# Filter rows of six group halves placed by DMA between SBUF rows instead of by one-hot products, with the evacuations shared out anew

## The chip, the cores and the metric

One NeuronCore of a Trainium2 chip runs the whole program. The metric is the time of one execution on the device, in microseconds (us), as the median of several runs. A trace of one further execution of each kernel gives its profile; its "span" is a little shorter than the timed execution. All runs are used unless they lie over 1.5% above the fastest of their kernel.

Engine names as in the profile: PE is the matrix engine (PEld its weight loads), DVE the vector engine, ACT the scalar engine, POOL is GpSimd, SP the sync engine, which here only issues DMA transfers (SPq is its queue).

## The reference

```python
# x: (8, 3072, 256); filt_r, filt_i: (1537, 256); w1, w2: (256, 1024); w_out: (1024, 256)
X = np.fft.rfft(x, axis=1)
Y = X * (filt_r + 1j * filt_i)[None, :, :]
y = np.fft.irfft(Y, n=3072, axis=1).reshape(24576, 256)
out = np.maximum(y @ w1, y @ w2) @ w_out
```

## The kernel before

Both Fourier transforms are products with tables, in two stages. The start-up does the forward transform of the first two batch items in eight rounds, one for each group of filter rows; then a long body interleaves the dense layers of one item with the transforms of the next. The change touches the start-up alone.

The filter rows lie in SBUF as `Fs` (96 partitions of 16 rows each), but the multiplication wants them in `F`, where partition 64c + 12q + j holds row 8j + 4b + c of `Fs`, and a partition 32 further on holds the mirrored row in reversed order. In the kernel before PE does this move: for each group `g` and part (real or imaginary) eight products with a one-hot matrix `Sel`, then an evacuation from PSUM to `F`, by ACT in one instruction or by DVE in two.

```python
    def expand_f(g, ri, E, sp=0):
        if E is V:
            pf = [p2.tile([128, 2, D], FP32, tag="px", name="pf", bufs=4) for _ in range(2)]
        else:
            p_ = bank2([128, 2, 2, D], FP32, "pf")
            pf = [p_[:, b] for b in range(2)]
        fs = Fs[ri]
        spin(pf[0].rearrange("p u d -> p (u d)"), sp)
        for b in range(2):
            for c in range(2):
                m = 4 * b + c
                TE.matmul(pf[b][64 * c:64 * c + 32], Sel[:, m], fs[:, 2 * g:2 * g + 2], start=True, stop=True)
                p0 = 64 * c + 32
                if g:
                    TE.matmul(pf[b][p0:p0 + 32], Sel[:, 7 - m], fs[:, 16 - 2 * g:14 - 2 * g:-1], start=True, stop=True)
                else:
                    TE.matmul(pf[b][p0:p0 + 32, 0], Sel[:, 7 - m + c], fs[:, 0], start=True, stop=True)
                    TE.matmul(pf[b][p0:p0 + 32, 1], Sel[:, 7 - m], fs[:, 15], start=True, stop=True)
        f_ = F[:, ri, :, 2 * g:2 * g + 2].rearrange("p b u d -> p b (u d)")
        if E is V:
            for b in range(2):
                V.tensor_copy(f_[:, b], pf[b].rearrange("p u d -> p (u d)"))
        else:
            evac(E, f_, p_.rearrange("p b u d -> p b (u d)"))
```

The eight rounds of the start-up. `first_t1` ends in the evacuation of a transpose ("T1"), `first_s2` makes the products `px` and multiplies them by `F` (`pq`), `first_s3` makes the products `pz`. `prep_wd` is the difference Wd = w1 - w2, which the first dense product `ph` needs.

```python
    load_f0()
    patch_f0()
    first_s1(5, S, 2)
    expand_f(6, 0, V)
    first_t1(1, V)
    first_t1(2, V)
    expand_f(1, 1, S)
    expand_f(7, 0, S)
    table_e(t1)
    pend = []
    for n, g in enumerate(order):
        pend.append(first_s2(g, n in (0, 1, 2, 4, 6)))
        if n < 6:
            first_t1(order[n + 2], V)
        if n == 0:
            tables_pe()
            expand_f(2, 1, S)
        if n < 6:
            expand_f((0, 3, 4, 5, 6, 7)[n], 1, S)
        if n < 2:
            load_x(1, 4 + n)
        if n == 2:
            fix_f()
        if n in (1, 3):
            tables_q(n // 2, S)
        if n in (4, 6):
            prep_wd(n // 2 - 2, *wf)
        if n in (4, 5):
            prep_w(n - 4, V)
        if n > 5:
            prep_w(n - 4, S)
        if n == 5:
            table_g()
        if n > 1:
            first_s3(*pend.pop(0))
    first_s3(*pend.pop(0))
    first_s3(*pend.pop(0), split=True)
# ... the body follows ...
```

## Time and profile before

| | before |
|---|---|
| time, median of 2 runs | 527.7 us (527.67 to 527.74) |
| profiled span | 523.8 us |
| PE busy, mean granted clock | 96% of the span, 0.999 |
| end of the last start-up multiplication on DVE | 43.94 us |
| first dense product `ph` on PE | 48.24 us |

From `ph` on, PE is the bound for the remaining 475 us, and nothing there is edited, so "when does the first `ph` start" measures the start-up with one number. The prediction below shows the lines of the profile from which this is read. In a line of a timeline the columns are: start, duration, engine, source line, operation, output<-inputs, shapes, count, and in brackets the idle time before it and what ended that. The first `ph` of the kernel before:

```profile
48.24 0.62 PE L596 MATMUL ph<-y__1134,Wd 128*128 128x512 bf16 x2 [0.38 <-ACT y__1134 L583]
```

### The profile page before, as it was taken

To read this page: it belongs to the slowest core of one execution; us is meant where nothing else is said; L and a number is where in the kernel's file an instruction comes from. 1 tells how busy PE (TensorE), PEld (TensorE's weight loads), DVE (VectorE), ACT (ScalarE), POOL (GpSimd) and SP (SyncE) were. 2 spreads that over 40 slices of the span, in tenths; PEclk is the share of its full clock that TensorE was granted. 3 is DMA by queue.
4 is the path that set the end of the run, shared out by engine and by line. 5 is a ranking of instruction groups with operands and counts; after the bars stand their busy time and mean duration, and the time that the engine had idled before them with its cause. 6 is when DMAs were issued, how large, how long until landed. Compare 5 with 4: busy or idle time off the path is not lost.

```text
span 523.8 us, 12526 instructions
## 1 busy us (share of the span) xinstructions
PE 504.0 (96%) x5204; PEld 346.5 (66%) x5282; DVE 322.4 (62%) x437; ACT 336.9 (64%) x597; POOL 148.0 (28%) x168
## 2 busy tenths in 40 slices
PE   8988989999999999999999999999999999999997
PEld 3556655666667766676666666676667666677775
DVE  8986567435773476437783588537783588544432
ACT  6786658746885588756675577647675556645542
POOL 6683118264027204530066002720000000000000
PEclk9999999999999999999999999999999999999999
DMA  7990699997798969796798769894467936341212
GB/s 143 280 204 23 176 199 320 334 204 177 232 247 241 208 195 300 229 200 185 219 266 201 182 179 241 266 202 139 143 172 157 176 111 150 100 125 41 82 62 100
DMA packets 74093, 97.03 MB, mean 185 GB/s; under 512 B 5106, under 2 KB 49780, under 8 KB 73044
## 3 DMA queue, kind: packets, MB, share of 16 engines
q1 hardware_dynamic: 63012, 63.72, 52.6%
q0 software_dynamic: 11024, 32.51, 20.1%
q8 instruction: 41, 0.67, 0.6%
q14 instruction: 16, 0.13, 0.1%
HBM read 54.79 MB, written 47.19 MB: 195 GB/s over the span
## 4 chain that ended last, share of the span: by engine, by line
PE 76%; issue 1%; DVE 1%; ACT 0%
PE po L621 30%; PE ph L596 26%; PE po L616 7%; PE pz L447 4%; PE py L580 3%; PE px L469 2%; PE pa L410 2%; DVE pq L474 0%; ACT at L413 0%; DVE ot L623 0%
## 5 line engine op out<-in xcount | busy, mean ns | idle before, releaser
L601 ACT ACTIVATE gt<-ph 128x512 bf16<-128x512 f32 x308 | 182.1, 603 | 125.5 <-PE ph L596 124.0
L621 PE MATMUL po<-Wo,gt 128*128 128x256 bf16 x1536 | 229.8, 273 | 3.4
L621 PEld LDWEIGHTS <-gt 128*128 128x128 bf16 x1536 | 150.2, 98 | 57.6
L474 DVE TENSOR_TENSOR pq<-px,F 120x1024 bf16<-120x1024 f32 x112 | 131.7, 1219 | 32.6 <-PE px L469 32.4
L623 DVE COPY ot<-po 128x512 f32<-128x512 f32 x96 | 66.2, 690 | 103.9 <-PE po L621 102.3
L628 POOL DMA_DIRECT2D out_dram<-ot x47 | 25.8, 548 | 311.0 <-DVE ot L623 298.8
L402 POOL TENSOR_TENSOR xd<-xf 128x512 bf16<-128x512 f32 x72 | 89.1, 1268 | 47.2 <-DMA xf<-in_x_dram 46.2
L596 PEld LDWEIGHTS <-Wd 128*128 128x128 bf16 x768 | 70.8, 98 | 21.2 <-issue 12.6
L451 ACT ACTIVATE zt<-pz 112x512 bf16<-112x512 f32 x112 | 61.0, 602 | 19.5 <-PE pz L447 16.4
L599 DVE TENSOR_SCALAR gt<-ph 128x512 bf16<-128x512 f32 x76 | 52.2, 687 | 29.4 <-PE ph L596 22.0
L413 ACT ACTIVATE at<-pa 128x512 bf16<-128x512 f32 x72 | 39.2, 596 | 15.6 <-PE pa L410 15.4
L580 PE MATMUL py<-G,zr 128*128 128x128 bf16 x384 | 30.1, 219 | 1.9 <-ACT zr L514 0.7
L447 PE MATMUL pz<-pq,VP 56*64 56x256 bf16 x448 | 29.4, 271 | 1.1 <-DVE pq L474 0.8
L580 PEld LDWEIGHTS <-zr 128*128 128x128 bf16 x384 | 25.3, 98 | 5.1 <-issue 3.6
L447 PE MATMUL pz<-pq,VQ 56*64 56x256 bf16 x448 | 28.6, 268 | 0.0
L469 PE MATMUL px<-bt,U 48*64 48x256 bf16 x448 | 23.5, 274 | 1.0 <-DMA bt<-ad 1.0
L469 PEld LDWEIGHTS <-U 48*64 48x64 bf16 x448 | 11.6, 106 | 9.2 <-issue 6.0
L447 PEld LDWEIGHTS <-VP 56*64 56x64 bf16 x448 | 14.1, 105 | 3.7 <-issue 2.4
L530 DVE TENSOR_TENSOR pq<-px,F 120x1024 bf16<-120x1024 f32 x11 | 13.2, 1222 | 3.5 <-ACT F L514 1.9
L410 PE MATMUL pa<-xd,C 64*64 64x512 bf16 x144 | 15.2, 400 | 0.0
L514 ACT ACTIVATE F<-pf 128x1024 bf16<-128x1024 f32 x10 | 10.1, 1032 | 6.7 <-PE pf L134 6.7
L447 PEld LDWEIGHTS <-VQ 56*64 56x64 bf16 x448 | 13.9, 106 | 0.0
(387 smaller groups left out, 591.2 us busy)
## 6 DMA issues: line engine op xcount, KB each, us to landing
out_dram<-ot POOLq DMA_DIRECT2D x47, 512.0 KB, 5.1
xf<-in_x_dram SPq DMA_DIRECT2D x72, 256.0 KB
ad<-at SPq DMA_DIRECT2D x42, 256.0 KB
bt<-ad SPq DMA_DIRECT2D x56, 192.0 KB
zd<-zt SPq DMA_DIRECT2D x56, 192.0 KB
zr<-zd SPq DMA_DIRECT2D x14, 768.0 KB
xb<-in_x_dram POOLq DMA_DIRECT2D x12, 256.0 KB, 10.6
wf<-in_moe_w_dram POOLq DMA_DIRECT2D x2, 1024.0 KB, 10.3
```

The costliest lines, as they stand in the source:

```text
L402: G.tensor_tensor(xb[b, c][:, i], xf[:, 0], xf[:, 1], op)
L413: S.activation(at[:, 2 * m:2 * m + 2], pa[m], AF.Copy)
L447: TE.matmul(pz[c][64 * k:64 * k + 64, i], W[64 * c:64 * c + 56, 2 * g + i, k], pq[k][64 * c:64 * c + 56, ri, i], start=(ri == 0), stop=(ri ...
L451: S.activation(zt[0:ROWS, c, o:o + 2], pz[c][0:ROWS], AF.Copy)
L469: TE.matmul(px[k][64 * c:64 * c + 64, i], U[64 * k:64 * k + 48, 4 * g + 2 * i + c], bt_[64 * k:64 * k + 48, t_], start=True, stop=True)
L474: V.tensor_tensor(pq[k][0:FROWS], px[k][0:FROWS].rearrange("p (o i) d -> p o i d", o=1).to_broadcast([FROWS, 2, 2, D]), F[0:FROWS, :, k, 2 ...
L580: TE.matmul(py[:, n], zr[b][:, 4 * i + n, 128 * dc:128 * dc + 128], G1, start=True, stop=True)
L596: TE.matmul(ph, Wd[:, dc, 128 * j:128 * j + 128], y_[:, dc].rearrange("p a b -> p (a b)"), start=(dc == 0), stop=(dc == 1))
L599: V.tensor_scalar(gt[tt][:, j], ph, 0.0, None, OP.max)
L601: S.activation(gt[tt][:, j], ph, AF.Relu)
L621: TE.matmul(p_, g_[:, jj, 128 * n:128 * n + 128], Wo[:, jj], start=False, stop=(jj == 7))
L623: V.tensor_copy(ot[tt][:, n - 1:n + 1], po[tt])
```

## The change

Its intent is to take work off PE, ACT and DVE in the start-up, where all three are nearly full, by letting the DMA engines place six of the sixteen group halves: imaginary rows of groups 4 to 7, real ones of 6 and 7. The rows that no transfer writes must be zero, hence two clears. The relief is then used to move three T1 evacuations from DVE to ACT and one Wd difference from GpSimd to DVE.

```diff
--- before.py
+++ after.py
@@ -141,6 +141,24 @@
                 V.tensor_copy(f_[:, b], pf[b].rearrange("p u d -> p (u d)"))
         else:
             evac(E, f_, p_.rearrange("p b u d -> p b (u d)"))
+
+    def spread_f(ri, g0):
+        n = 16 - 2 * g0
+        for b in range(2):
+            for c in range(2):
+                m = 4 * b + c
+                for q in range(2):
+                    p0 = 64 * c + 12 * q
+                    nc.sync.dma_start(out=F[p0:p0 + J, ri, b, 2 * g0:16], in_=Fs[ri][m:m + 89:8, 2 * g0:16])
+                    nc.sync.dma_start(out=F[p0 + 32:p0 + 32 + J, ri, b, 2 * g0:16],
+                                      in_=Fs[ri][7 - m:96 - m:8, n:0:-1])
+
+    def clear_f(ri, g0, E):
+        f_ = F[:, ri, :, 2 * g0:16].rearrange("p b u d -> p b (u d)").bitcast(FP32)
+        if E is S:
+            S.activation(f_, zero.rearrange("p (a b) -> p a b", a=1).to_broadcast([128, 2, (16 - 2 * g0) * D // 2]), AF.Copy)
+        else:
+            E.memset(f_, 0.0)
 
     F0 = zpool.tile([64, 2, 2, D], FP32, tag="zt", name="F0")
 
@@ -201,6 +219,7 @@
                         fill=1.0 - 2.0 * q, base=-12 * (1 - q), channel_multiplier=1)
     load_x(0, 4)
     load_x(0, 5)
+    clear_f(0, 6, G)
     load_f(1)
 
     Ct = init.tile([128, 128], BF16)
@@ -337,8 +356,8 @@
         for _ in range(n):
             TE.matmul(pd, Sp, Sp.rearrange("p (o x) -> p o x", o=1).to_broadcast([128, 4, 128]), start=True, stop=True)
 
-    def prep_wd(k, w1f, w2f):
-        G.tensor_tensor(Wd[:, k], w1f[:, k], w2f[:, k], OP.subtract)
+    def prep_wd(k, E, w1f, w2f):
+        E.tensor_tensor(Wd[:, k], w1f[:, k], w2f[:, k], OP.subtract)
 
     def load_wo():
         G.dma_start(out=Wo, in_=moe_w_out.rearrange("(c p) j -> p c j", p=128))
@@ -644,6 +663,7 @@
     zeros(At[:, :, 48:64].rearrange("p h m t -> p h (m t)"), [4, 512])
     zeros(U.rearrange("p t (q x) -> p (t q) x", q=2)[:, :, 24:32], [64, 8])
     zeros(VP.rearrange("p u b n -> p (u b) n")[:, :, 48:64], [32, 16])
+    clear_f(1, 4, S)
     bt[0] = bpool.tile([128, T, D], BF16, tag="bt", name="bt")
     uu, mk, t1 = tables_u()
     done = []
@@ -671,30 +691,32 @@
     load_f0()
     patch_f0()
     first_s1(5, S, 2)
-    expand_f(6, 0, V)
+    expand_f(1, 1, S)
     first_t1(1, V)
     first_t1(2, V)
-    expand_f(1, 1, S)
-    expand_f(7, 0, S)
+    spread_f(1, 4)
+    spread_f(0, 6)
+    expand_f(2, 1, S)
     table_e(t1)
     pend = []
     for n, g in enumerate(order):
         pend.append(first_s2(g, n in (0, 1, 2, 4, 6)))
         if n < 6:
-            first_t1(order[n + 2], V)
+            first_t1(order[n + 2], (V, S)[n > 2])
         if n == 0:
             tables_pe()
-            expand_f(2, 1, S)
-        if n < 6:
-            expand_f((0, 3, 4, 5, 6, 7)[n], 1, S)
+        if n < 2:
+            expand_f((3, 0)[n], 1, S)
         if n < 2:
             load_x(1, 4 + n)
         if n == 2:
             fix_f()
-        if n in (1, 3):
-            tables_q(n // 2, S)
-        if n in (4, 6):
-            prep_wd(n // 2 - 2, *wf)
+        if n in (1, 2):
+            tables_q(n - 1, S)
+        if n == 3:
+            prep_wd(0, V, *wf)
+        if n == 6:
+            prep_wd(1, G, *wf)
         if n in (4, 5):
             prep_w(n - 4, V)
         if n > 5:
```

## The prediction

> **What bounds the kernel now.** I read the engine rows of the page first, then the chain that ended last, then the busy time by stage, then the timelines of the vector engine and of the sync engine's DMA queue in the first 48 us, where the whole change lies.
>
> ```profile
> span 523.8 us, 12526 instructions
> PE 504.0 (96%) x5204; PEld 346.5 (66%) x5282; DVE 322.4 (62%) x437; ACT 336.9 (64%) x597; POOL 148.0 (28%) x168
> PE po L621 30%; PE ph L596 26%; PE po L616 7%; PE pz L447 4%; PE py L580 3%; PE px L469 2%; PE pa L410 2%; DVE pq L474 0%; ACT at L413 0%; DVE ot L623 0%
> ```
>
> From about 114 us to the end the chain is almost nothing but PE (L621, L596, L616: the dense layers). Nothing in that body is edited. The first dense product (ph, L596) starts at 48.24 us in the PE timeline, and the stretches of 50 us after 100 us show PE busy for 48.9 and 49.2 of 50. So the start-up before 48 us can only move the end by moving the moment at which the body starts, and then nearly one for one.
>
> The start-up by stage (columns: stretch, length, busy PE, PEld, DVE, ACT, POOL, granted clock, DMA share, GB/s):
>
> ```profile
> 20.00:30.00 10.00, 8.95 (x163) 5.32 (x157) 7.96 (x15) 8.22 (x11) 7.55 (x8) 1.00 1.12 299
> 30.00:40.00 10.00, 9.00 (x194) 5.51 (x194) 9.10 (x11) 8.16 (x11) 8.42 (x6) 1.00 1.05 186
> 40.00:47.00 7.00, 5.57 (x160) 3.95 (x159) 4.22 (x5) 4.12 (x6) 4.45 (x2) 1.00 0.01 2
> ```
>
> DVE and ACT are both close to full from 20 to 40 us. Just as important: the DMA engines are saturated (1.12, 1.05) until the records of the software queue end at 39.66 us, and idle afterwards. The chain through this stage is eight rounds (groups in the order 1, 2, 3, 4, 5, 0, 6, 7) of products px, multiplication by the filter on DVE (L530), products pz:
>
> ```profile
> 29.92 2.36 DVE L530 TENSOR_TENSOR pq<-px,F 120x1024 bf16<-120x1024 f32 x2 [0.51 <-ACT F L514]
> 33.40 1.22 DVE L530 TENSOR_TENSOR pq<-px,F 120x1024 bf16<-120x1024 f32 x1 [0.53 <-ACT VQ L514]
> 36.20 2.36 DVE L530 TENSOR_TENSOR pq<-px,F 120x1024 bf16<-120x1024 f32 x2 [0.37 <-issue]
> 41.58 2.36 DVE L530 TENSOR_TENSOR pq<-px,F 120x1024 bf16<-120x1024 f32 x2 [0.70 <-issue]
> ```
>
> The first line is group 4: it needs its filter rows at 29.92. The last is group 7; its end, 43.94, releases the last pz and then the body. What feeds it by one-hot products costs, per group and part, an ACT evacuation:
>
> ```profile
> L514 ACT ACTIVATE F<-pf 128x1024 bf16<-128x1024 f32 x10 | 10.1, 1032 | 6.7 <-PE pf L134 6.7
> ```
>
> The queue on which the new transfers will go shows how small transfers fare while the engines are saturated:
>
> ```profile
> 18.59 2.31 SPq L154 DMA_DIRECT2D F<-in_filt_r_dram  x6
> 20.94 5.21 SPq L154 DMA_DIRECT2D F<-in_filt_i_dram  x6
> 27.77 0.24 SPq L157 DMA_DIRECT2D F<-in_filt_i_dram  x1
> 28.06 0.25 SPq L158 DMA_DIRECT2D F<-in_filt_r_dram  x1
> SPq L154 <- DMA F<-in_filt_r_dram: 3.3, 4, 2.2
> ```
>
> An issue takes 0.24 to 0.4 us, yet the second six took 5.21. In the built program each transfer of this queue waits for the one eight places earlier, and the ninth indeed starts only at 23.85: the first, issued at 18.59, took 5.2 us to land. By the trace's records of single DMA packets its first packet ran at 22.16, 3.5 us after the issue. The two patches, issued at 27.77 and 28.06, have their packets at 31.37 and 31.68, 3.6 us after.
>
> **What the Trainium skill says.** "Perfetto Trace Analysis", DMA Instruction, HWDGE: the profiled time ends when the sequencer has pushed the transfer; movement is not in it. The trace agrees (0.43 us shown, 5.2 us to landing). "DMA: Bandwidth & Descriptors", Queues, rings and completion order: a DMA engine goes round the queues that have work, packet by packet. The trace agrees: from 22.2 us each engine took a packet of this queue about every 0.22 us, one software packet of 4096 bytes (185 ns) and one of its own (some 50 ns). Same page, Why a DMA increments its semaphore by 16: the number of engines divides the slowest dimension; 12 rows make 12 engines, one row each. "TensorE: Matmul & The Clock Gate", Part 1: after an idle window of about 3.4 us the PE clock halves until it has been busy that long. No such gap is in this trace (clock 1.00 throughout).
>
> **The change part by part.** Removed: six expansions. On PE two of them ran from 19.86 to 20.74, so 0.44 each, 2.6 us in all. ACT loses five evacuations, at 0.92 from start to start, 4.6 us; DVE loses two copies of some 0.6, 1.2 us. Moved: three T1 evacuations from DVE to ACT (DVE -1.8, ACT +2.8), one Wd difference from POOL (2.35) to DVE (about 1.25, from the 0.96 of the 768-wide difference at L275). Added: a clear on ACT of about 1.9 us (At's zeros are 2048 wide and took 1.89), which fits into ACT's idle 2.17 us before 9.78; and a memset on POOL, which fits in its later idle 1.76 us. On those engines alone it is a net saving of up to 2 or 3 us.
>
> Also added: 32 transfers on the sync queue, and the changed program's order puts them behind load_f0 and the patches. So none is issued before 28.3 us. Group 4 multiplies at 29.92 today; in the changed program its first half waits for the eight imaginary transfers with b = 0, its second half and the GpSimd half of group 5 for the eight with b = 1. My working of these:
> - Issues. 1 to 6 at 28.35 to 30.1 (their predecessors land by 29.8). Number 7 waits for the first patch (31.6), number 8 for the second (32.0).
> - Service. First packets about 3.5 us after the issue, 32.1. A forward transfer is 1 row of 4 KB and a completion per engine, 2 turns; a reversed one is 8 pieces of 512 bytes and a completion, 9 turns. Four pairs are 44 turns; at 0.21 us (software packets of 2048 bytes, 173 ns, plus some 40) that is 9.2 us: the first eight land at about 41.
> - Second eight. Numbers 9 to 15 queue behind; 16 can only be issued when 8 has landed, 41.5, and lands near 43. Even at no service time, 16 cannot land before 32.0 + 3.7 + 3.7, about 39.5.
> - The sixteen real ones, then on idle engines at some 0.3 us each, land by about 48 at the latest, before groups 6 and 7 (below) want them.
>
> DVE from the second half of group 4 at 43: itself 1.15, Wd 1.25, group 5 1.15, w2T 0.6, group 0 2.3, w2T 0.6, group 6 1.15, a gap of 0.75 for group 7's px (as today), group 7 2.35: 11.3 us, end at 54.3. Today that stretch ran from 31.06 to 43.94, 12.9 us. So the saving is 1.5 us and the wait costs 12: **+10.4 us**. On top, PE will have stood idle some 10 us while DVE waits; if its clock halves, the transposes, w2T and pz work between groups 4 and 0 (about 2 us warm, starting 44.2) grows to about 3.6 and delays group 0 by some 1.4. Sum about +12, so 527.7 + 12 = 539.7; I put 539.5.
>
> **The rivals.**
> (1) The transfers are hidden, and the relief counts. For it: ACT's waits and the 0.51 us wait for F before group 4 go. Against it: the issue after 28.3 and the latency above. It would give about 525.
> (2) The transfers stall DVE but are served faster, eight pieces in one packet: first eight at 37, sixteenth at 41, PE stays warm: +7 to +9, about 535 to 537. For it: packet records cannot tell how many pieces one turn takes.
> (3) My main case, +10 to +14.
> (4) Worse: 512-byte pieces from SBUF to SBUF are slow to issue or land, and the real rows for groups 6 and 7 hold DVE a second time: +16 or more, 544 and up. Nothing in this trace measures an SBUF-to-SBUF transfer.
>
> **Range and chances.** The 2% line is 527.7 x 1.02 = 538.3, between rival 2 and the main case. I give rival 1 0.06, rival 2 0.36, main 0.43, worse 0.15. Range 533 to 546. Faster by over 2% (below 517.1) would need more than 10 us out of a 48 us start-up: 0.01. Slower 0.58, the rest same, 0.41.
>
> **What would show it.** In the profile after: a wait on DVE before the pq multiplication of the fourth round, named with a DMA F<-Fs, of 9 to 13 us; spread issues starting at about 28.3 with gaps from the seventh; PE idle some 10 us from about 31 and a granted clock below 1.00 just after; the first ph product at 58 to 61 instead of 48.24; the spacing from there to the end unchanged. The prediction is wrong if the spread transfers land within 2 or 3 us under load, if DVE waits for something else, or if the later body gives time back.

## The result

| | before | after |
|---|---|---|
| time, median of 2 runs | 527.7 us (527.67 to 527.74) | 549.5 us (549.35 to 549.73) |
| profiled span, mean clock | 523.8 us, 0.999 | 547.2 us, 0.975 |
| last start-up multiplication on DVE ends | 43.94 us | 60.83 us |
| first `ph` | 48.24 us | 67.79 us |

The kernel became slower: ratio 1.0414, 95% interval 1.0369 to 1.0459. Ratios in this document are the mean time of one kernel's fast runs over that of the other's of the same rounds, so not quite the ratio of the medians that are quoted. The predicted class was right; the predicted time (539.5, range 533 to 546) was 10 us too low.

The page of the kernel after, its span, its engine rows, the granted clock in 40 slices, and the chain that ended last by engine:

```profile
span 547.2 us, 12569 instructions
...
PE 511.6 (94%) x5234; PEld 348.5 (64%) x5234; DVE 323.5 (59%) x433; ACT 336.6 (62%) x596; POOL 146.4 (27%) x168
...
PEclk9885799999999999999999999999999999999999
...
PE 77%; DMA 14%; SPq 4%; ACT 2%; DVE 1%; POOL 1%; issue 1%; POOLq 0%; ACTq 0%
```

The chain now runs through DMA transfers and, for 4% of the span (22 us), through SPq: through the *issuing* of transfers. The clock dips in slices 2 to 5 (14 to 68 us) and is full afterwards. The same by stage (stretch, length, busy PE, PEld, DVE, ACT, POOL, clock, DMA share, GB/s):

```profile
30.00:40.00 10.00, 6.41 (x149) 4.61 (x149) 0.97 (x2) 6.29 (x9) 5.21 (x6) 0.91 1.09 214
40.00:50.00 10.00, 1.00 (x8) 0.44 (x8) 4.58 (x4) 0.00 (x0) 2.12 (x1) 0.50 0.23 53
50.00:60.00 10.00, 8.24 (x153) 5.69 (x152) 7.31 (x8) 4.77 (x7) 0.39 (x1) 0.73 0.11 29
60.00:70.00 10.00, 6.75 (x93) 4.62 (x94) 3.59 (x6) 3.97 (x7) 4.04 (x2) 0.66 0.06 21
```

From 40 to 50 us nearly everything stands still, the DMA engines too (share 0.23). So it is not bandwidth that is missing there. DVE's timeline shows what it waits for:

```profile
42.40 1.23 DVE L549 TENSOR_TENSOR pq<-px,F 120x1024 bf16<-120x1024 f32 x1 [10.40 <-DMA F<-Fs]
46.64 1.22 DVE L549 TENSOR_TENSOR pq<-px,F 120x1024 bf16<-120x1024 f32 x1 [3.02 <-DMA F<-Fs]
47.78 2.08 DVE L360 TENSOR_TENSOR Wd<-wf 128x1024 bf16<-128x1024 f32 x1
...
59.60 1.23 DVE L549 TENSOR_TENSOR pq<-px,F 120x1024 bf16<-120x1024 f32 x1 [1.21 <-DMA F<-Fs]
```

The first two lines are group 4's halves (imaginary rows), the last is group 7's second half (real rows). GpSimd, which multiplies its share of groups 5 and 7, waits for the same transfers, 21.2 us in two waits:

```profile
L549 POOL TENSOR_TENSOR pq<-xs,F 120x1024 bf16<-120x1024 f32 x5 | 10.7, 2137 | 23.8 <-DMA F<-Fs 21.2
```

And the sync queue shows where those transfers are:

```profile
21.18 2.24 SPq L172 DMA_DIRECT2D F<-in_filt_r_dram  x6
23.46 4.61 SPq L172 DMA_DIRECT2D F<-in_filt_i_dram  x6
...
30.11 0.86 SPq L152 DMA_DIRECT2D F<-Fs  x1
31.08 0.88 SPq L153 DMA_DIRECT2D F<-Fs  x1
...
36.11 0.81 SPq L153 DMA_DIRECT2D F<-Fs  x1
...
38.83 0.74 SPq L152 DMA_DIRECT2D F<-Fs  x1
40.46 0.82 SPq L153 DMA_DIRECT2D F<-Fs  x1
...
43.76 0.82 SPq L153 DMA_DIRECT2D F<-Fs  x1
...
57.13 0.82 SPq L153 DMA_DIRECT2D F<-Fs  x1
```

The lines shown of the spread are numbers 1, 2, 8, 11, 12, 16 and 32. The queue issues them one after the other from 30.11 to 57.95, with one real gap: 0.89 us before number 12, which by the profile waits for an earlier transfer of the spread to land (number 4, if each waits for the one eight places earlier, as the prediction read from the program). That is 27.8 us for 32, so 0.87 each, where I had reckoned with 0.3. Compare issue ends and waits: number 8 has been issued by 36.92 and its rows are there at 42.40, 5.5 us later; number 16 by 44.58 and there by 46.64, 2.1 us later; number 32 by 57.95, and the multiplication that needs it starts at 59.60, 1.7 us later. The software queue with the weights and x has its last packet at 40.44. So the first wait ends late because of slow landing *and* slow issue, the second mostly because of slow issue, and the last because of slow issue alone. How much of the second is issue can be estimated from these numbers: had issuing cost nothing, number 16 would still have waited for number 8, there at 42.40, and landed some 2 us later, at 44.4 instead of 46.64, so about 2.2 us of it are issue.

```profile
67.79 1.06 PE L615 MATMUL ph<-y__1106,Wd 128*128 128x512 bf16 x2
```

The body starts at 67.79, 19.55 us later than before, and its first two products take 1.06 us where they took 0.62: PE is still at the low clock.

### The profile page after: what moved, and what is told of

Its sections match the earlier page's. It is cut to its first block, busy times and chain, and to the rows that moved or that the text cites. A ratio compares the mean times of both kernels' runs of the same rounds, so it can differ in the third digit from the quotient of the medians.

```text
span 547.2 us, 12569 instructions
## 1 busy us (share of the span) xinstructions
PE 511.6 (94%) x5234; PEld 348.5 (64%) x5234; DVE 323.5 (59%) x433; ACT 336.6 (62%) x596; POOL 146.4 (27%) x168
## 4 chain that ended last, share of the span: by engine, by line
PE 77%; DMA 14%; SPq 4%; ACT 2%; DVE 1%; POOL 1%; issue 1%; POOLq 0%; ACTq 0%
PE ph L615 29%; PE po L640 28%; PE po L635 7%; PE pz L466 4%; PE py L599 4%; DMA zd<-zt 3%; DMA Wo<-in_moe_w_out_dram 2%; PE px L488 2%; PE pa L429 2%; DMA xb<-in_x_dram 2%; DMA F<-Fs 2%; SPq L153 2%; DMA xf<-in_x_dram 2%; SPq L152 2%; DMA zr<-zd 1%; DMA bt<-ad 1%
## 5 line engine op out<-in xcount | busy, mean ns | idle before, releaser
L615 PEld LDWEIGHTS <-Wd 128*128 128x128 bf16 x768 | 70.9, 98 | 21.2 <-issue 12.7
L549 POOL TENSOR_TENSOR pq<-xs,F 120x1024 bf16<-120x1024 f32 x5 | 10.7, 2137 | 23.8 <-DMA F<-Fs 21.2
```

What stands on the lines that cost most here:

```text
L615: TE.matmul(ph, Wd[:, dc, 128 * j:128 * j + 128], y_[:, dc].rearrange("p a b -> p (a b)"), start=(dc == 0), stop=(dc == 1))
```

## The experiments

My theory after reading the result, called I below: a transfer from SBUF to SBUF is itself dear to issue, and 32 in a row on one queue set when the rows are there. The main rival, L: the transfers land late because the DMA engines are full, and the issue hardly matters. (The expectations of the first two batches have letters of their own, which each text explains.) Smaller suspects: the GpSimd memset at the start, the cold PE clock, and the new sharing of evacuations. Twelve kernels ran. In the table, "`ph`" is the start of the first `ph` against the 48.24 us of the kernel before, from the profile; the times are medians with the kernel before of the same chip beside them.

| kernel | us | before | ratio (95%) | `ph` |
|---|---|---|---|---|
| after | 549.5 | 527.7 | 1.041 (1.037 to 1.046) | +19.55 |
| e_imag_only | 542.7 | 527.6 | 1.027 (1.024 to 1.031) | +14.24 |
| e_memset_late | 548.4 | 527.6 | 1.039 (1.035 to 1.042) | +17.91 |
| e_reshare | 529.0 | 527.6 | 1.003 (0.998 to 1.007) | +0.60 |
| e_quiet | 550.0 | 527.1 | 1.043 (1.039 to 1.046) | +20.04 |
| e_early | 546.7 | 527.1 | 1.037 (1.034 to 1.039) | +16.43 |
| e_warm | 548.9 | 527.1 | 1.040 (1.037 to 1.044) | +18.59 |
| v_best | 532.3 | 527.1 | 1.010 (1.008 to 1.013) | +4.63 |
| e_dram | 549.7 | 528.7 | 1.042 (1.036 to 1.047) | +18.68 |
| v_dram | 553.5 | 528.7 | 1.045 (1.041 to 1.049) | +20.77 |
| e_two | 548.1 | 529.6 | 1.036 (1.031 to 1.041) | +17.66 |
| e_free (wrong result) | 528.7 | 529.6 | 1.002 (0.994 to 1.009) | -1.00 |

### p_issue: what one issue costs

The kernel before, with some 30 transfers on the sync queue behind its last output, when the compute engines have finished. It is timed by its trace alone (its one run took 549.8 us, the added transfers included).

```diff
+    for r in range(4):                                       # rows 8 apart, as the change has them
+        nc.sync.dma_start(out=F[32*r:32*r + J, 0, 0, 8:16], in_=Wo[r:r + 89:8])
+    # the same with adjacent rows, reversed rows, from DRAM, from DRAM reversed,
+    # and with 16, 96 and 128 rows
```

> The kernel before, with some 30 transfers of like size added on the sync queue behind the last output, so that the DMA engines are idle and each issue is seen by itself. The result stays correct. Theory A (an issue from SBUF to SBUF is itself dear): 12 rows with the source stepping 8 partitions take 0.74 us (forward) and 0.81 us (reversed), as in the changed kernel; 12 adjacent rows take the same; 12 rows from DRAM take about 0.3 us, reversed or not. Rival A2 (the step over 8 partitions is what costs): adjacent rows take about 0.3 us, stepped ones 0.74. Rival A3 (12 rows, a count that is not a power of two, cost): 16 rows take 0.3, and 12 rows 0.74 from DRAM as well.

The answers for these source lines (count, then minimum/median/maximum in ns). In order: SBUF to SBUF, 12 rows 8 apart; 12 adjacent rows; 12 reversed; DRAM to SBUF, 12 rows; the same reversed; SBUF to SBUF with 16 rows; with 128 rows; SBUF to DRAM, 12 rows:

```profile
L791 SPq DMA_DIRECT2D F<-Wo x4: 714/734/867, 525.2 to 527.6; - x4
...
L794 SPq DMA_DIRECT2D F<-Wo x4: 713/714/714, 528.4 to 530.7; - x4
...
L797 SPq DMA_DIRECT2D F<-Wo x4: 782/792/859, 531.4 to 534.0; - x4
...
L800 SPq DMA_DIRECT2D F<-fd x4: 342/362/537, 534.8 to 536.2; - x4
...
L803 SPq DMA_DIRECT2D F<-fd x4: 364/372/373, 536.6 to 537.9; - x4
...
L806 SPq DMA_DIRECT2D F<-Wo x4: 582/592/606, 538.3 to 540.2; - x4
...
L807 SPq DMA_DIRECT2D F<-Wo x1: 595/595/595, 540.8 to 540.8; - x1
...
L811 SPq DMA_DIRECT2D fd<-Wo x4: 364/588/1441, 542.1 to 544.8; - x4
```

With no other traffic than these transfers themselves (only the first four still ran beside the write of the copy in DRAM) a 12-row transfer from SBUF to SBUF takes 0.71 to 0.79 us to issue, and one of the same shape from DRAM 0.36 to 0.37. The step of 8 partitions adds almost nothing (734 against 714), the reversal 0.06 to 0.08. More rows are not dearer: 16 rows took 0.592, 128 rows 0.595. It is not the source alone that counts, though: with DRAM at the other end an issue out of SBUF was as short as 0.364, and v_dram below has issues out of DRAM of 0.76. So the 0.3 us of my prediction, taken from transfers out of DRAM, was the wrong row to read. The 0.74 and 0.81 us of the kernel after are thus the price of the transfer itself.

### e_imag_only and e_memset_late: the real rows, and the memset

e_imag_only leaves the imaginary transfers and places the real rows of groups 6 and 7 by products again, so it needs no memset on GpSimd either. e_memset_late is the changed kernel with that memset moved from about 7 us to just ahead of the spread.

```diff
 # e_imag_only
-    clear_f(0, 6, G)
+    expand_f(6, 0, V)
-    spread_f(0, 6)
+    expand_f(7, 0, S)
 # e_memset_late: this line moved behind first_t1(2, V)
-    clear_f(0, 6, G)
+    clear_f(0, 6, G)
```

> The changed kernel, but the real rows of groups 6 and 7 by one-hot products again: 16 transfers, not 32. Theory A (the sync engine issues one after the other, 0.82 us each, and that sets when rows are there): the wait before group 4's second half stays, near 46 us less some 2 us because the memset on GpSimd is gone too; the wait before the last multiplication (59.60 in the changed kernel) and the one on GpSimd go; end of the start-up some 5 to 7 us earlier, 541 to 545 us in all. Rival B (the wait before group 4 is all that matters, and the later waits are only its shadow): the time stays at 548 to 550.

> The changed kernel, with the GpSimd memset of F moved from before the second filter's loads to just before the spread, some 15 us later. Theory C (the memset holds up DVE at 7 us, this makes PE wait and its clock fall at 14 us, and this delays load_f0 and with it all 32 issues): DVE's waits at 5.4 to 8.1 us go, the clock stays at 1.00 from 10 to 20 us, the first spread issue comes at 28.4 in place of 30.1 us, and the time falls by 1.5 to 2.5 us. Rival: the dip of the clock is a matter of chance in this run, and the time stays within 0.5 us.

DVE's waits in e_imag_only, then in e_memset_late:

```profile
42.59 1.23 DVE L548 TENSOR_TENSOR pq<-px,F 120x1024 bf16<-120x1024 f32 x1 [13.89 <-DMA F<-Fs]
45.25 1.23 DVE L548 TENSOR_TENSOR pq<-px,F 120x1024 bf16<-120x1024 f32 x1 [1.43 <-DMA F<-Fs]
```

```profile
42.66 1.23 DVE L548 TENSOR_TENSOR pq<-px,F 120x1024 bf16<-120x1024 f32 x1 [12.90 <-DMA F<-Fs]
45.55 1.23 DVE L548 TENSOR_TENSOR pq<-px,F 120x1024 bf16<-120x1024 f32 x1 [1.66 <-DMA F<-Fs]
...
58.41 1.23 DVE L548 TENSOR_TENSOR pq<-px,F 120x1024 bf16<-120x1024 f32 x1 [0.77 <-DMA F<-Fs]
```

In both, the first wait ends where it ended in the changed kernel (42.40), although the spread starts 1.5 us earlier (28.55 and 28.62). That speaks for L on the first wait: what is issued while the engines are full is served no sooner. The second wait ends 1.1 to 1.4 us sooner. The wait before group 7 is there only with the real transfers. The forecast for e_imag_only held (541 to 545 us, measured 542.7). Between the two kernels, both without an early memset, `ph` differs by 17.91 - 14.24 = 3.7 us: that is the cost of the sixteen real transfers.

The memset cost 19.55 - 17.91 = 1.6 us at `ph`, read from one trace of each; the times do not show it (ratios of 1.041 and 1.039, with intervals that overlap). How, the start of the changed kernel shows:

```profile
7.12 0.95 DVE L281 TENSOR_SCALAR kb<-kb,col 128x24 f32<-128x24 f32 x1
...
13.71 0.38 PE L131 MATMUL pf<-Fs,Sel 96*32 96x512 bf16 x1 [1.43 <-DVE F L141]
```

While GpSimd clears (7.06 to 8.03), a DVE instruction of 24 columns takes 0.95 us; it took 0.24 in the kernel before. DVE comes 1.65 us late to its evacuations, PE waits, its clock falls (0.83 between 10 and 20 us, 1.00 in e_memset_late) and load_f0, on which the spread queues, starts at 21.18 instead of 18.59. A like hold of about 1.0 us stands a little before the memset's own record in all six kernels that have the memset there, and in none of the others; why it starts before the record stays open (the profile's own note calls spans on GpSimd rough). The second hold, at 7.1 us, is there in only four of the six: in e_quiet and e_free DVE is some 0.5 us late, the clock is 1.00 from 10 to 20 us, and e_quiet's load_f0 starts at 19.07. So the memset does not cost the same in every run.

### e_reshare: the new sharing alone

```diff
 # on the kernel before
-            first_t1(order[n + 2], V)
+            first_t1(order[n + 2], (V, S)[n > 2])
-        if n in (4, 6):
-            prep_wd(n // 2 - 2, *wf)
+        if n == 3:
+            prep_wd(0, V, *wf)
+        if n == 6:
+            prep_wd(1, G, *wf)
```

> The kernel before, with only the other half of the change: T1 evacuations of later rounds on ACT, the first Wd difference on DVE. No transfers, all expansions by one-hot products. If the sharing out by itself costs nothing: within 1 us of before, 527 to 529. If ACT, which keeps its evacuations of F here, becomes the bound of the start-up, or if Wd on DVE is held by GpSimd (2.08 us in the changed kernel in place of 1.25): 1 to 3 us slower. In no case the 22 us of the change.

The same within the noise, with `ph` 0.6 us later. The sharing is not what costs. Its Wd on DVE took 1.31 us, close to my estimate of 1.25; in the changed kernel it took 2.08, because there it runs beside GpSimd's multiplication at 46.66, which had waited for the same transfer.

### e_quiet: the load taken away

The six loads of x that crowd the engines until 40 us are moved behind the fifth round.

```diff
-    for c in range(4):
-        load_x(1, c)
-        if n < 2:
-            load_x(1, 4 + n)
+        if n == 4:
+            for c in range(6):
+                load_x(1, c)
```

> The changed kernel, with the six loads of the second batch's x (1.5 of 7.9 MB of the software queue) moved from 18 to 30 us behind GpSimd's multiplication of group 5 (46 us), so that the DMA engines are free from about 33 us on. Theory A (issues one after the other on the sync engine set the end): the first half of group 4 waits less (until about 39.5 in place of 42.4), the second half and the last multiplication wait as long as before (to 46.6 and 59.6, each within 1 us), and the time stays within 1.5 us of the change's. Rival T2 (landing under traffic): all three waits end 3 us or more earlier and the time falls by 3 us or more.

Issues 8 and 16 of the sync queue, and DVE's waits:

```profile
34.95 0.82 SPq L153 DMA_DIRECT2D F<-Fs  x1
...
41.54 0.81 SPq L153 DMA_DIRECT2D F<-Fs  x1
```

```profile
37.80 1.23 DVE L549 TENSOR_TENSOR pq<-px,F 120x1024 bf16<-120x1024 f32 x1 [9.13 <-DMA F<-Fs]
44.39 1.23 DVE L549 TENSOR_TENSOR pq<-px,F 120x1024 bf16<-120x1024 f32 x1 [5.37 <-DMA F<-Fs]
...
54.87 2.36 DVE L549 TENSOR_TENSOR pq<-px,F 120x1024 bf16<-120x1024 f32 x2 [2.66 <-DMA F<-Fs]
...
59.88 1.23 DVE L549 TENSOR_TENSOR pq<-px,F 120x1024 bf16<-120x1024 f32 x1 [2.65 <-DMA F<-Fs]
```

Here both theories can be told apart. Without load number 8 lands 2.0 us after its issue ends (35.77 to 37.80) and number 16 too (42.35 to 44.39). So 3.5 of the 5.5 us that landing took in the changed kernel are load, and L is right for the first wait, which ends 4.6 us sooner (1.2 of it the earlier start of the queue). But the second wait ends only 2.3 us sooner, and it does so because the queue started 1.2 us earlier and had no gap: 16 issues take 13.4 us even without load (14.5 in the changed kernel, the gap included). Theory I is right for the second wait and for what is behind it in the changed kernel. (To the letter neither forecast was met: the second wait's end moved by more than theory I's 1 us and less than the rival's 3.) The total did not fall, since the x loads, now at 46 us, made the real rows late in turn (54.87 and 59.88).

### e_early: the transfers issued earlier

The loads of F0 and all 32 spreads stand at the start, both clears on ACT.

```diff
+    V.memset(F0[:, :, :, 0:1], 0.0)     # at about 1 us, removed from its later place
+    load_f0()
+    patch_f0()
...
-    clear_f(0, 6, G)
...
+    clear_f(0, 6, S)
+    spread_f(0, 6)                      # from 11.4 us, removed from their later place
+    spread_f(1, 4)
```

> All 32 transfers of the change, but issued earlier: the group-0 rows (F0) are loaded at the very start, the real rows are spread as soon as the real filter has landed (9 us), the imaginary ones right behind. Both clears are on ACT. Theory A (the sync engine needs about 0.83 us per transfer, one after the other): issues run from about 9.3 to 36 us; the eighth imaginary one is issued near 29 and lands by 36, the last near 36 and lands by about 41, so DVE waits before group 4 until about 41 in place of 46.6, and not at all before groups 6 and 7. Body start some 9 to 10 us later than before in place of 20, about 536 to 539. Rival T2 (it is the landing under the weights' traffic that sets the waits, not the issue): the earlier ones meet more of that traffic, and the wait ends at 44 or later, 541 or more.

```profile
40.14 1.23 DVE L551 TENSOR_TENSOR pq<-px,F 120x1024 bf16<-120x1024 f32 x1 [10.97 <-DMA F<-Fs]
46.44 1.23 DVE L551 TENSOR_TENSOR pq<-px,F 120x1024 bf16<-120x1024 f32 x1 [5.07 <-DMA F<-Fs]
```

The expectation of theory I was missed; that of its rival, the landing under load (a wait until 44 or later, 541 us or more), was met. All 32 were issued by 40.66, 17 us sooner than in the changed kernel, and still the second wait ended at 46.44: the last landed 5.8 us after its issue. The software queue, whose last packet was at 40.44 in the changed kernel, ran until 45.04 here. Issued earlier, the transfers share the DMA engines with the loads and lengthen them, and so the loaded time in which they land slowly. What remains is a gain of about 3 us at `ph`, the missing wait before group 7 and the missing memset.

### e_warm: the clock kept up

```diff
-        spin(pz[0], 1)
+        spin(pz[0], warm)     # 45 idle products in DVE's wait at group 4, 14 while it waits at group 7
```

> The changed kernel with idle products added on PE while it waits: 45 before the pz products of the fifth round, 14 before those of the seventh. Theory D (the halved PE clock after the stalls is a cost of its own, above all in the last steps from 62 us on, which lie on the path): the granted clock stays near 1.00 from 38 to 48 and from 60 to 68 us, the time from the last multiplication (59.6) to the first dense product falls from 8.2 to about 6 us, and the kernel gets 1.5 to 2.5 us faster. Rival: these steps are bound by latency and other engines, and the time stays within 0.7 us.

The clock stood at 1.00 from 30 to 50 us and from 60 to 70, against 0.91, 0.50 and 0.66, and the waits were the same (42.71, 46.32 and 59.47). `ph` came 1.0 us earlier than in the changed kernel. So the halved clock is a real but small part; the total did not move measurably (the forecast was 1.5 to 2.5 us).

### e_dram: the same transfers, cheap to issue

The 32 transfers as they are, but reading a copy of the rows in DRAM, written there by two transfers ahead of load_f0.

```diff
+        fd[ri] = dram.tile([96, 16, D], BF16, tag="fd%d" % ri, name="fd", bufs=1)
+        nc.sync.dma_start(out=fd[ri], in_=Fs[ri])
...
-                    nc.sync.dma_start(out=F[p0:p0 + J, ri, b, 2 * g0:16], in_=Fs[ri][m:m + 89:8, 2 * g0:16])
+                    nc.sync.dma_start(out=F[p0:p0 + J, ri, b, 2 * g0:16], in_=fd[ri][m:m + 89:8, 2 * g0:16])
```

> The changed kernel, but the same 32 transfers of 12 rows read a copy of the filter rows in DRAM (one write of each part, ahead of load_f0 on the same queue) instead of the copy in SBUF. Theory I (the dear issue of an SBUF-to-SBUF transfer, 0.71 to 0.87 us, sets when the rows are there): each issue falls to 0.36 to 0.4 us, sixteenth issued near 39 (held by the lanes, not by issue), waits before group 4 end at about 39 and 43, none before group 7; first ot copy +12 to +14 over before; total about 540, as my prediction said. Theory L (the landing under the load of the other queues sets it, issue time hardly matters): the waits end at about 42.5 and 46.5 as in the changed kernel, only the one before group 7 goes; about 545. If the two writes of 0.75 MB crowd the engines before 40 us, the first wait may end a few us later than either theory says.

```profile
36.16 0.30 SPq L158 DMA_DIRECT2D F<-fd  x1
36.49 0.37 SPq L159 DMA_DIRECT2D F<-fd  x1
...
53.45 0.37 SPq L159 DMA_DIRECT2D F<-fd  x1
```

```profile
46.97 1.23 DVE L555 TENSOR_TENSOR pq<-px,F 120x1024 bf16<-120x1024 f32 x1 [14.36 <-DMA F<-fd]
49.94 1.23 DVE L555 TENSOR_TENSOR pq<-px,F 120x1024 bf16<-120x1024 f32 x1 [1.74 <-DMA F<-fd]
```

The issue fell to 0.29 to 0.37 us, and the wait before group 7 for rows is gone. But the copies made the engines fuller (the software queue ended at 44.77), and the spread only began at 36.16, 6 us later, so the total stayed. As a test of the total the run is thus inconclusive; its intervals are not. From the first issue to the start of group 4's two halves it took 10.8 and 13.8 us; in the changed kernel 12.3 and 16.5. With cheap issues the queue is held by the landings instead (number 7 and later are issued with gaps). So on the first wait the dear issue costs about 1.5 us over what the load alone would make of it, on the second 2.7: an estimate, since the load of the two kernels isn't the same.

### e_two: two queues

The eight reversed imaginary transfers are issued by ACT's DMA queue, one or two at a time between its evacuations from 21.3 us, the rest by the sync queue.

```diff
-                    nc.sync.dma_start(out=F[p0 + 32:p0 + 32 + J, ri, b, 2 * g0:16], ...)
+                    nc.scalar.dma_start(out=F[p0 + 32:p0 + 32 + J, ri, b, 2 * g0:16], ...)   # imaginary ones
```

> The changed kernel with the eight reversed imaginary transfers issued by the scalar engine's DMA queue, one or two at a time between its evacuations from about 24 us, the other 24 on the sync queue as before. Same bytes, same sources, same load. Theory I (serial issue): the sync queue has issued its eight imaginary ones by 36.5 instead of 44.6 and its last real one by 50 instead of 58; first wait ends about 40.5 (landing under load), second about 41.5, none before group 7; first ot copy +14; total 541 to 543. Theory L (landing): waits end at 42.4 and 46.5 again, total within 2 us of the changed kernel. Each issue may cost the scalar engine 0.8 us, which could delay VQ and so the px of group 4 by up to 5 us; then the wait is named PE px.

The waits ended at 41.78, 44.62 and 57.94, between the two theories: 0.6, 2.0 and 1.7 us sooner. The sync queue began its part only at 33.31, 3.2 us later than in the changed kernel, and needed 10.24 us for its first nine transfers of the spread, waits among them, so that two queues together issued little faster than one. I take it that transfers of both wait for each other's landings, as those of one queue wait for the one eight places earlier, but did not check it; the run separates the theories less well than e_quiet does.

### e_free: the most that the change could win

The changed kernel without its 32 transfers, so that those rows are the zeros of the clears.

```diff
-    spread_f(1, 4)
-    spread_f(0, 6)
```

> Wrong result on purpose: the changed kernel without its 32 transfers, so that the imaginary rows of groups 4 to 7 and the real ones of 6 and 7 are the zeros of the two clears. It shows what the change could win at most, had the rows come for nothing. If the start-up is bound by the evacuations that the change takes away (my rival 1): 524 to 526, first ot copy 2 to 3 us before that of the kernel before. If other waits hold the eight rounds (the x loads, PE, the multiplications, the held-up DVE start): 527 to 529, within 1 us of the kernel before.

```profile
40.53 2.36 DVE L549 TENSOR_TENSOR pq<-px,F 120x1024 bf16<-120x1024 f32 x2 [0.64 <-PE px L540]
```

Had the rows come for nothing, the last multiplication would end at 42.89 instead of 43.94 and `ph` would come 1.0 us earlier; the time is the same as before within the noise. This speaks against my rival 1: even the full relief on PE, ACT and DVE is worth about 1 us of `ph` here (read from one trace, with the early memset in it; the interval of the times, 0.994 to 1.009, would allow anything from 3 us faster to 5 us slower). DVE's multiplications then wait for `px` on PE instead. The transfers therefore cost 19.55 + 1.00 = 20.6 us at `ph` to win 1.

### v_best and v_dram: attempts at a better version

v_best takes F0 early, spreads only groups 6 and 7 (both parts, from 11.3 us) and leaves groups 4 and 5 and Wd as before. v_dram copies the rows to DRAM early and spreads from there with 12 transfers for each part.

```diff
 # v_best, against the changed kernel
-    spread_f(1, 4)
+    spread_f(1, 6)                       # with spread_f(0, 6), early
+            expand_f((0, 3, 4, 5)[n], 1, S)
 # v_dram, against the changed kernel
+    save_f(0, 6)                         # SBUF to DRAM
+    save_f(1, 4)
+    spread_f(1, 4)                       # ahead of load_f0; b = 0 and 1 in one transfer where not reversed
```

> A version meant to beat both kernels: as e_early, but only groups 6 and 7 are spread by transfers, imaginary and real, those of 4 and 5 by one-hot products as before; T1 evacuations on ACT only in rounds 4 and 5, Wd on GpSimd as before. Theory A: issues from 9.3 to 36 us, the last lands near 40, when GpSimd's and DVE's halves of group 6 and 7 want them (40.0 and 42.7), so no wait for F<-Fs over 0.5 us on DVE. DVE loses two T1 copies (1.2 us) and ACT two evacuations of F in the last rounds: body start 0.5 to 1.5 us earlier than before, 526 to 527.5. If a wait for F<-Fs remains, 528 to 531.

> A version meant to use the change well: rows copied to DRAM as soon as they are in SBUF, then spread from there with 12 transfers for each part instead of 16 (both batch halves in one where the order of rows allows it), imaginary ones ahead of load_f0, real ones where the changed kernel has them, both clears on ACT. Theory I: imaginary issues take about 5 us in all and end before 25, landed by 30, no wait before group 4; real ones issued 29 to 35, landed by 40; total 524 to 529, at or just below the kernel before. Theory L: landing under load takes 5 to 7 us after issue all the same, a wait of 1 to 4 us before group 4, total 529 to 534. The extra 1.5 MB written may delay the x loads and so the first T1 evacuation, as early transfers did before.

In v_best the last of the 32 had been issued by 39.5 and landed near 44.4, again under load:

```profile
44.47 1.23 DVE L551 TENSOR_TENSOR pq<-px,F 120x1024 bf16<-120x1024 f32 x1 [2.63 <-DMA F<-Fs]
```

It is the best of the kernels with transfers, and 1% slower than the kernel before; both its forecasts (526 to 527.5, or 528 to 531 with a wait left) were too low. v_dram is the worst of all, against forecasts of 524 to 534: its copies, issued by about 24 us, went through full engines, so that the first spread was issued at 30.94, load_f0 behind them at 43.69, and DVE resumed at 49.90 after 19 us. Its forward transfers, each with both halves b in one, are also a warning about the issue: they read DRAM and still took 0.76 us each (the median of eight).

```profile
30.94 0.90 SPq L157 DMA_DIRECT2D F<-fd  x1
...
54.38 0.76 SPq L157 DMA_DIRECT2D F<-fd  x1
```

After e_free there was little reason to look further: with the work shared out as here, even free transfers would beat the kernel before by about 1 us.

## Why the prediction was right or wrong

**The bound and the mechanism: right.** The body bounds the program, and the start-up moves its end nearly one for one. The rows come late, DVE waits before group 4 (predicted 9 to 13 us, measured 10.40 and 3.02), PE stands idle and its clock halves (0.50 from 40 to 50 us). Rival 1 (hidden transfers, 525) and rival 2 (served sooner, PE warm) did not happen. That the class came out right is not luck: the imaginary transfers alone, on which the forecast of a loss rested, made e_imag_only slower by 2.7%. What happened is rival 4, to which I gave 0.15. The clear on ACT took its 1.89 us in ACT's idle time, as said.

**The step that failed is the issue, and behind it the real rows.** "The sixteen real ones, then on idle engines at some 0.3 us each, land by about 48 at the latest": they were issued from 44.68 to 57.95, at 0.74 to 0.82 us each, and group 7's second half started at 59.60. p_issue (0.71 to 0.79 us) shows that this is the price of the operation itself, not of the load. The estimate came from a transfer out of DRAM, and the prediction did say that nothing in the trace measured an SBUF-to-SBUF one; it should have weighted that gap more than at 0.15.

The terms of the sum, at the places where they can be read:

| step of the prediction | predicted | measured |
|---|---|---|
| first spread issued | 28.35 | 30.11 (memset on GpSimd, clock) |
| first half of group 4 | about 41 | 42.40 |
| second half of group 4 | about 43 | 46.64 |
| from there to the end of DVE's multiplications, cold clock included | 11.3 + 1.4 = 12.7 | 60.83 - 46.64 = 14.2 |
| first `ph` | 58 to 61 | 67.79 |

(In the prediction's sum for this stretch the saving is 12.9 - 11.3 = 1.6 us, not 1.5; its +10.4 us is right.) The second half's 3.6 us are 1.8 of late start and about as much of dear issue. The next row's 1.5 us are the Wd of 2.08 instead of 1.25 and the wait of 1.21 before group 7, less small gains. The rest, up to `ph`, is the tail behind DVE, for which I had only the 4.3 us of today (43.94 to 48.24): it took 7.0. Of these 2.7 us more, 0.9 are GpSimd's half of group 7, which waits for the same rows and ends at 61.73, after DVE; about 0.8 are the cold PE (clock 0.66; with the clock kept up, e_warm's tail was 6.1); the rest was not traced. Checked on the chip, the real rows are worth 3.7 us at `ph` (e_memset_late less e_imag_only), the memset 1.6, the cold clock about 1.0 (e_warm).

**The landing model held better than its inputs.** I had 12.65 and 14.65 us from the first issue to the two halves of group 4. The changed kernel measured 12.3 and 16.5. With issues as cheap as I had assumed, e_dram measured 10.8 and 13.8, under a load that isn't quite the same. If that carries over, the first figure came out so near in part by luck: the landing was reckoned some 1.9 us too slow, and the dear issue that I had left out added 1.5. Slow landing under load alone would thus have made most of the +12 that I predicted. That is an estimate; no run had cheap issues under the same load.

**"A memset on POOL, which fits in its later idle 1.76 us": wrong in its effect.** It fits on GpSimd (7.06 to 8.03), but it holds DVE.

**"The spacing from there to the end unchanged": open.** The median times rose by 0.8 to 4.1 us more than `ph` in the kernels whose body starts 14 us or more late (2.3 in the changed kernel: 21.8 less 19.55), and by 0.1 to 0.8 in e_reshare, v_best and e_free. In the changed kernel the profile shows some 2.7 us of it early in the body, at waits for transfers of the intermediate arrays. But p_issue, whose body is that of the kernel before instruction for instruction, lost 3.2 us between 109 and 118 us of its profiled run (by the copies `ot`), a stretch in which the changed kernel lost 1.6, and the kernel before varied from 526.1 to 532.3 us over the chips. Whether a late start costs the body something, or this is variation between runs, these runs do not settle.

## What to carry to other kernels

Before replacing compute by transfers, ask how many issues the queue must make in a row and measure one issue of just that kind, source and destination included; 32 short transfers between SBUF rows were 27 us of one queue, however idle the DMA engines were. Ask next under which load they land, because an earlier issue into full engines only shares the same time out anew. And try the version in which the replaced work is simply gone, with a wrong result: here it would have shown at once that the prize was about 1 us.

## What the Trainium skill lacked or had wrong

- "DMA: Bandwidth & Descriptors" gives a first-byte latency and a fixed cost of some 2 us for one transfer (Latency and other measured facts). For the time that one transfer occupies the issuing queue it has only a cycle count for "previous generations", in its part on trn3, and nothing on how that depends on where the transfer reads and writes. Measured: SBUF to SBUF 0.71 to 0.79 us for 12 rows and 0.595 for 128, DRAM to SBUF 0.36 to 0.37 for 12 (0.76 for 12 rows with two halves each, in v_dram). The 2 us are near what a transfer on quiet engines took: 2.0 in e_quiet from the end of its issue, 2.85 from its start, although no DRAM is touched; under load it was 5.5 us from the end of the issue.
- "SBUF — State Buffer", Who interferes with whom, says that two SBUF inputs on the vector engine contend with a GpSimd instruction that reads SBUF, and that `tensor_scalar` can hold or wait for the shared ports. The runs agree: Wd on DVE took 2.08 to 2.11 us beside GpSimd's multiplication and 1.22 to 1.31 otherwise, and a `tensor_scalar` 0.95 us instead of 0.24 beside the memset's record. What it does not give is the hold of about 1.0 us that stood before the memset's record in all six runs with it.
